# Column means of w1 from one summed block: three adds on GpSimd, one product per quarter, and a later load of w2

## The chip, the cores and the metric

The kernel runs on one core of a Trainium2 chip. The metric is the device time in microseconds (us), median of several runs; less is better. A core has TensorE (matrix products), VectorE, ScalarE, GpSimd, and SyncE, whose queue issues the DMAs of this kernel. In the profile they are called PE, DVE, ACT, POOL and SP (SPq for the queue); PEld is the loading of TensorE's weights.

## The reference

The program is a layer with a long convolution (part A) followed by a two-layer perceptron (part B), over 2048 tokens of 512 columns, in bf16:

```python
def _A_ref(q, k, v, shift_k, ssm_k, ssm_D):
    # k_shift: causal 4-tap filter of k; kv = k_shift * v
    # y: causal convolution of kv with ssm_k, 2048 long, by FFT of length 4096
    y = y + kv * ssm_D[None, None, :]
    return q * y
def _B_ref(x, w1, w2):                       # w1: 512 x 1376, w2: 1376 x 512
    h = jnp.maximum(jnp.einsum("bsd,df->bsf", x, w1), 0)
    return jnp.einsum("bsf,fd->bsd", h, w2)
x = A_q
h = x + _A_ref(_layernorm(x, axis=-1), A_k, A_v, A_shift_k, A_ssm_k, A_ssm_D)
h2 = h + _B_ref(_layernorm(h, axis=-1), B_w1, B_w2)
```

The second layernorm is not applied to h by the kernel. Its subtraction of the mean is moved into the weights: from each column of `w1` the mean of that column over the 512 rows is taken off. Its division is applied at the end, per token. The column means of `w1` are what this change is about.

## The kernel before

The convolution is done with matrix products: a two-stage forward transform of the filter and of kv, a product in the transformed domain, and a two-stage inverse. The span falls into these stretches:

- 0 to 30 us: loading, tables of sines, taps of k, first stages of the transforms.
- 30 to 61 us: second stage for the filter, first stage for kv.
- 61 to 92 us: `product(kp)` for 16 values of kp, each with `finish` two steps behind. VectorE and GpSimd share the multiplications (L452), ScalarE copies, TensorE combines them in `psy` (L462). The result is `kf`.
- 92 to 110 us: inverse stage 1, `inv1(b)` for b = 0 to 15. Each b is 16 small products (L609) into `psi`, which one engine then copies to `ax` (L259 on ScalarE, L261 on VectorE; VectorE has b = 5 and 10 and half of the last). `psi` has three places in PSUM, used in a ring, so block b can begin when the copy of block b-3 is done.
- From 110 us: inverse stage 2 (`inv2_first`, `inv2`, result `pz`), `gate` (times the normed x, plus x, L660 and L662), and the perceptron, `mlp1(sc)` (L716) and `mlp2(sc)` (L746) for four groups sc of 512 tokens. The products of `inv2` for the next groups are slipped in between those of `mlp1` and `mlp2`.

Each engine takes its instructions strictly in the order of the program, since the schedule is written by hand. The order of the calls in the text is thus the order of the queues. What stands around the change:

- `load_x(q)` brings the tokens of group q into `xh[q]`; `lift(q)` transposes them to `xT[q]` by DMA. `ln1_stats(q)` computes mean and variance of each token on VectorE (`st` L547, `mv` L551) and from it `rstd` in two steps on GpSimd (L553, L554). `ln1_norm(q)` applies both on VectorE in four instructions (`qln`, L571) and sends the result through a transposing DMA to `qT[q]`.
- `ec_turns(q)` computes angles on GpSimd (one iota, L526, and two multiplications, L529); `ec_wrap(q)` reduces them on VectorE (L533); sines of them on ScalarE give `ecore0` (for group 0) and `bd` (L537, for the others), both operands of inverse stage 2.
- `column_means(n)` for n = 0 to 3 multiplies a 128x128 block of 1/512 in bf16, `ones`, with a quarter of the columns of `w1` (344 of 1376). `w1` lies as four row blocks of 128 rows, so a quarter takes four products that add up in PSUM in `cen[n]` (tile `pm`, L497). n = 0 and 1 stand in front of inverse stage 1, n = 2 after b = 9, n = 3 after b = 15.
- `center` subtracts the means from `w1` (L578): quarters 0 and 1 on VectorE after b = 5, quarters 2 and 3 on GpSimd, which gets the means by way of `wm`.
- `load_w2` brings `w2` by two DMAs (L590, L592), after `lift(0)` and before inverse stage 1. `w2` takes the place of the table `c2n1`, which the last `product` reads last.

Of the kernel before, what the change touches and what calls it, by code (L numbers as in the profile page):

```python
# [9 lines left out]
ALU = mybir.AluOpType  # L10
BF16 = mybir.dt.bfloat16
F32 = mybir.dt.float32
F32R = mybir.dt.float32r
I32 = mybir.dt.int32
PSUM = bass.MemoryType.PSUM
P = 128
# [40 lines left out]
def kernel(  # L57
# [13 lines left out]
    nc = tc.nc  # L71
    _, S, D = A_q.shape
    DFF = B_w1.shape[1]
# [3 lines left out]
    DC = D // P  # L77
    NFC = (DFF + P - 1) // P
# [10 lines left out]
    wp = pl.push("wp", side="right")  # L89
# [49 lines left out]
    def _sin(out, turns, M, neg=False):  # L139

        nc.scalar.activation(out=out, in_=turns, func=ACT.Sin, scale=(-TURN if neg else TURN) / M,
                             bias=(pbias if neg else nbias)[:])
# [94 lines left out]
    for rg in range(DC):  # L237
        nc.gpsimd.tensor_tensor(out=wdiag[:, rg, :, :], in0=ident[:].unsqueeze(1).to_broadcast([P, KS, P]),
                                in1=wsh[:, rg, :].unsqueeze(2).to_broadcast([P, KS, P]), op=ALU.mult)
# [152 lines left out]
    ones = consts.tile([P, P], BF16, name="ones")  # L392
# [64 lines left out]
    def finish(at):  # L457
        kp, (tr, ti) = pending.pop(0)
        for s, (a, b, m) in enumerate(((tr[:, 0], ti[:, 1], ineg), (tr[:, 1], ti[:, 0], ipos))):
            psy = psy_.tile([P, 512], F32, tag=f"psy{s}", name=f"psy{s}")  # L460
            for m_, t_, first in ((ipos, a, True), (m, b, False)):
                nc.tensor.matmul(out=psy[:], lhsT=m_[:], rhs=t_.rearrange("p j k -> p (j k)"),  # L462
                                 start=first, stop=not first)
            copy("D" if at == 16 and s == 1 else "A", kf[:, s, :, 2 * kp:2 * kp + 2],
                 psy[:].rearrange("p (j k) -> p j k", k=2))
# [9 lines left out]
    for kp in range(16):  # L475
# [6 lines left out]
        if kp == 10:  # L482
            w1 = wp.tile([P, DC, DFF], BF16, tag="c2s0", name="w1")
# [5 lines left out]
    psum1 = pl.push("psC", space=PSUM)  # L489
    psum_a = pl.push("psIa", space=PSUM)  # L490
    FS = 344
    cen = {}

    def column_means(n):
        cen[n] = psum1.tile([P, 512], F32, tag=f"pm{n % 2}", name="pm")
        for c in range(DC):
            nc.tensor.matmul(out=cen[n][:, 0:FS], lhsT=ones[:], rhs=w1[:, c, n * FS:(n + 1) * FS],  # L497
                             start=(c == 0), stop=(c == DC - 1))

    while pending:  # L500
        finish(16)
    column_means(0)
    column_means(1)
    pl.pop("psY")
    places[:] = [psum_a] + [pl.push("psIb", side="right", space=PSUM)] * 2
    ring[:] = [0, 1, 2]
# [10 lines left out]
    rstd2 = late.tile([P, NT, 1], F32, name="rstd2")  # L517
    ecw = [late.tile([P, 2, 512], I32, name="ecw0"), wp.tile([P, 2, 512], I32, tag="c2s1", name="ecw1")]
    ecore0 = wp.tile([P, 2, 16, 32], F32R, tag="c2n0", name="ecore0")
    w2 = wp.tile([P, NFC, D], BF16, tag="c2n1", name="w2")  # L520
    bd = [late.tile([P, 2, 8, DC, 32], F32R, name="bd0")]
    act_pool = {0: late}

    def ec_turns(q):
        t = ecw[q % 2]
        nc.gpsimd.iota(t[:, 1, :].rearrange("p (i a n) -> p i a n", i=4, a=4), pattern=[[1, 4], [16, 4], [64, 32]],  # L526
                       base=4 * q, channel_multiplier=0)
        for rho, o in enumerate((2048 + 4096, 8192)):
            nc.gpsimd.tensor_scalar(out=t[:, rho, :], in0=t[:, 1, :], scalar1=k1o[:], scalar2=float(o),  # L529
                                    op0=ALU.mult, op1=ALU.add)  # L530

    def ec_wrap(q):
        nc.vector.tensor_single_scalar(out=ecw[q % 2][:], in_=ecw[q % 2][:], scalar=8191, op=ALU.bitwise_and)  # L533
# [22 lines left out]
    def rows_T(dst, src):  # L556
        nc.sync.dma_start_transpose(out=dst[:].rearrange("p i r t -> p (i r) t"),
                                    in_=src.rearrange("p i d -> p (i d)"))

    def lift(q):  # L560
        xT[q] = act_pool[q].tile([P, 4, DC, P], BF16, name=f"xT{q}")
        rows_T(xT[q], xh[q])

    def ln1_stats(q, part=slice(0, 4)):
        stats(xh[q], mv1, rstd1, q, part)

    def ln1_norm(q):
        qln = late.tile([P, 4, D], BF16, tag="qln", name="qln", bufs=1)
        for i in range(4):
            t = 4 * q + i  # L570
            nc.vector.tensor_scalar(out=qln[:, i, :], in0=xh[q][:, i, :], scalar1=mv1[:, t, 0:1],  # L571
                                    scalar2=rstd1[:, t, :], op0=ALU.subtract, op1=ALU.mult)
        qT[q] = act_pool[q].tile([P, 4, DC, P], BF16, name=f"qT{q}")
        rows_T(qT[q], qln[:])

    def center(eng, n, mean):
        fs = slice(n * FS, (n + 1) * FS)
        eng.tensor_tensor(out=w1[:, :, fs], in0=w1[:, :, fs], in1=mean.unsqueeze(1).to_broadcast([P, DC, FS]),  # L578
                          op=ALU.subtract)
# [4 lines left out]
    def off_center(n):  # L584
        nc.vector.tensor_copy(out=wm[:, n - 2, :], in_=cen[n][:, 0:FS])
        center(nc.gpsimd, n, wm[:, n - 2, :])

    def load_w2():
        nfull = DFF // P
        nc.sync.dma_start(out=w2[:, 0:nfull, :], in_=B_w2[0:nfull * P, :].rearrange("(c p) d -> p c d", p=P))  # L590
        if DFF % P:
            nc.sync.dma_start(out=w2[0:DFF % P, nfull, :], in_=B_w2[nfull * P:DFF, :])  # L592

    ec_turns(0)
    ln1_stats(0)
    ec_turns(1)
# [2 lines left out]
    def inv1(b):  # L599
        if b < 15:  # L600
            ps = bank2("psi1")
            banks = (ps[:, 0], ps[:, 1])
        else:
            banks = (psum1.tile([P, 512], F32, tag="pm0", name="psi1a")[:], bank2("psi1b")[:, 0, :])
        for i in range(4):
            m = 4 * b + i
            for c, tab in ((0, dre), (1, dim)):
                for dp in range(2):
                    nc.tensor.matmul(out=banks[dp][:, 128 * i:128 * i + 128],  # L609
                                     lhsT=kf[halves[dp], c, 4 * m:4 * m + 4, :].rearrange("p r k -> p (r k)"),  # L610
                                     rhs=tab[halves[dp], dp].rearrange("p a b -> p (a b)"), start=(c == 0), stop=(c == 1),
                                     tile_position=(64 * dp, 0), skip_group_check=True)
        if b < 15:
            copy("D" if b in (5, 10) else "A", ax[:, :, :, 4 * b:4 * b + 4],
                 ps[:].rearrange("p d (i x) -> p x d i", i=4))
        else:
            for dp, eng in enumerate("AD"):
                copy(eng, ax[:, :, dp, 60:64], banks[dp].rearrange("p (i x) -> p x i", i=4))

    lift(0)  # L620
    load_w2()
    ec_wrap(0)
    ln1_stats(1, slice(0, 2))
    for b in range(16):
        inv1(b)
        if b == 4:
            ln1_norm(0)
            _sin(ecore0[:].rearrange("p b j n -> p b (j n)"), ecw[0][:], 8192)
        if b == 5:
            center(nc.vector, 0, cen[0][:, 0:FS])  # L630
            ln1_stats(1, slice(2, 4))
            center(nc.vector, 1, cen[1][:, 0:FS])
        if b == 7:
            ec_turns(2)
        if b == 9:
            column_means(2)
        if b == 10:
            off_center(2)
            ec_wrap(1)
    column_means(3)  # L640
    nc.vector.tensor_copy(out=wm[:, 1, 1:FS], in_=cen[3][:, 1:FS])
    nc.vector.tensor_copy(out=wm0[:], in_=cen[3][:, 0:1])
    bd_sins(1, 0)
# [200 lines left out]
```

## Time and profile before

| what | value |
|---|---|
| median of 3 runs | 204.63 us (204.31 to 205.11) |
| profiled execution: its own time | 203.83 us |
| profiled execution: span from first to last instruction | 201.7 us |
| granted TensorE clock, mean | 0.995 |
| PE busy | 192.0 us, 95% of the span |
| DVE busy | 145.3 us, 72% |
| ACT busy | 128.5 us, 64% |
| POOL busy | 86.5 us, 43% |
| column means on PE, L497 | 16 products of 128x344, 91.8 to 109.3 us |
| centring on POOL, L578 | 2 of 128x1376, mean 2844 ns |
| centring on DVE, L578 | 2 of 128x1376, mean 1559 ns |
| rstd on POOL, L554 | 8, mean 1036 ns |
| w2's DMAs | issued at 95.7 and 96.5 us, 1280 and 96 KB |

The busy figures are averages over stretches with different limits. A busy time of PE includes products that are pipelined, so it does not say that PE works at its peak. What a change in one stretch is worth is read from the chain of work that ended last, in that stretch: it follows back, from the last instruction, what released each step.

### The profile page before, as it was taken

Reading aid. Unit: us, or ns where it says so; the run is one execution under the profiler, and the core shown is the slowest. Engines: PE = TensorE matmul, PEld = TensorE weight load, DVE = VectorE, ACT = ScalarE, POOL = GpSimd, SP = SyncE. Lnnn points to the kernel's source line nnn. Section 1 sums busy time; section 2 is a strip of 40 time slices with the busy share of each in tenths; the row PEclk is TensorE's granted clock in tenths of the full one; section 3 lists DMA queues with packets and bytes.
Section 4 is the critical chain, followed back from the end, with each engine's and each line's share of the span. In section 5 each row is a group of like instructions: output and inputs, shape, how many; then the busy total and the mean of one; then the engine's idle time right before and its main releaser. Section 6 shows DMA issues by size and latency. Waiting matters only on the chain.

```text
span 201.7 us, 5574 instructions
## 1 busy us (share of the span) xinstructions
PE 192.0 (95%) x2337; PEld 135.5 (67%) x2337; DVE 145.3 (72%) x238; ACT 128.5 (64%) x199; POOL 86.5 (43%) x121
## 2 busy tenths in 40 slices
PE   7799999999988999999999999999999999999991
PEld 2465555999977998987988877545664556544451
DVE  7998777887887998898994798968477127661131
ACT  2668899678785888885979865925570683036300
POOL 7599994000016999994959293301120002002000
PEclk9999999999999999999999999999999999999998
DMA  6999991000000007719981989744381702140011
GB/s 164 349 221 181 165 180 27 3 5 3 6 3 2 0 23 196 272 28 209 275 190 28 113 77 199 141 99 106 82 156 57 104 0 52 35 96 28 0 52 52
DMA packets 48492, 20.06 MB, mean 99 GB/s; under 512 B 43380, under 2 KB 46932, under 8 KB 48468
## 3 DMA queue, kind: packets, MB, share of 16 engines
q1 hardware_dynamic: 47940, 19.71, 48.1%
q8 instruction: 18, 0.29, 0.6%
q10 hardware_dynamic: 528, 0.00, 0.1%
q14 instruction: 6, 0.05, 0.1%
HBM read 7.08 MB, written 2.10 MB: 46 GB/s over the span
## 4 chain that ended last, share of the span: by engine, by line
PE 69%; SPq 10%; DVE 8%; DMA 5%; ACT 3%; issue 1%; POOL 1%; ACTq 0%
PE ps1m L716 19%; PE ps2m L746 19%; PE psy L462 6%; PE ps2k L328 4%; DMA kT<-in_A_k_dram 4%; SPq L115 4%; PE ps2k L330 4%; PE u L328 4%; PE u L330 3%; SPq L118 3%; SPq L117 3%; PE pz L689 3%; PE ps L310 2%; PE pst L281 2%; PE pkv L369 2%; DVE st L547 2%
## 5 line engine op out<-in xcount | busy, mean ns | idle before, releaser
L731 ACT ACTIVATE h1T<-ps1m 128x512 bf16<-128x512 f32 (+1 forms) x44 | 25.7, 597 | 35.8 <-PE ps1m L716 35.7
L716 PE MATMUL ps1m<-xT,w 128*128 128x512 bf16 (+2 forms) x192 | 43.7, 365 | 0.4 <-DVE xT L662 0.4
L746 PE MATMUL ps2m<-w,h1T 128*128 128x512 bf16 (+3 forms) x187 | 40.8, 368 | 0.0
L689 PE MATMUL pz<-bd,ax 128*128 128x128 f32 x96 | 35.7, 410 | 0.0
L452 POOL TENSOR_TENSOR t<-usb,kf 128x320 fp32r<-128x320 f32 x32 | 28.2, 930 | 2.2 <-ACT usb L448 1.7
L452 DVE TENSOR_TENSOR t<-u,kf 128x704 fp32r<-128x704 f32 x32 | 26.7, 884 | 3.3 <-ACT usb L448 3.2
L750 DVE SCALAR_TENSOR_TENSOR o<-ps2m,rstd,xh 128x512 bf16<-128x512 f32 (+1 forms) x17 | 12.1, 717 | 22.4 <-PE ps2m L746 11.5
L553 POOL TENSOR_SCALAR rstd<-mv 128x4 f32<-128x4 f32 x8 | 2.5, 317 | 57.1 <-DVE mv L551 57.1
L746 PEld LDWEIGHTS <-h1T 128*128 128x128 bf16 (+1 forms) x187 | 16.2, 98 | 16.0
L259 ACT CAST a<-ps 128x1024 fp32r<-128x1024 f32 (+1 forms) x22 | 22.4, 1053 | 2.8 <-PE ps L310 2.8
L716 PEld LDWEIGHTS <-w 128*128 128x128 bf16 (+1 forms) x192 | 15.9, 100 | 12.1 <-DVE xT L662 0.5
L689 PEld LDWEIGHTS pz<-bd,ax 128*128 128x128 f32 x96 | 18.6, 193 | 7.6
L547 DVE BATCH_NORM_STATS2 st<-xh 128x6 f32<-128x512 bf16 x32 | 19.9, 677 | 0.4 <-DMA xh<-xT 0.4
L660 DVE TENSOR_TENSOR qT<-pz,qT 128x1024 bf16<-128x1024 f32 x8 | 9.8, 1220 | 13.6 <-PE pz L689 10.8
L259 ACT CAST kf<-psy 128x512 fp32r<-128x512 f32 x30 | 17.5, 642 | 1.9 <-PE psy L462 0.2
L537 ACT ACTIVATE bd<-ecw,nbias 32x512 fp32r<-32x512 int32 x24 | 17.3, 719 | 0.6
L462 PE MATMUL psy<-t,ipos 128*128 128x512 f32 x48 | 16.0, 393 | 0.0
L369 PE MATMUL pkv<-kT,wdiag 128*128 128x512 bf16 x64 | 15.2, 380 | 0.6 <-POOL f_lo L247 0.4
L261 DVE CAST a<-ps 128x1024 fp32r<-128x1024 f32 (+1 forms) x12 | 13.6, 1136 | 2.7 <-PE ps L310 2.5
L259 ACT CAST ax<-psi 128x1024 fp32r<-128x1024 f32 x13 | 12.3, 1038 | 3.7 <-PE psi L609 3.5
L372 DVE TENSOR_TENSOR sk<-pkv,vT 128x512 bf16<-128x512 f32 x16 | 10.7, 689 | 4.5 <-PE pkv L369 4.1
L609 PE MATMUL psi<-dre,kf 64*128 64x128 f32 x120 | 13.8, 274 | 0.1
(132 smaller groups left out, 401.6 us busy)
## 6 DMA issues: line engine op xcount, KB each, us to landing
sk<-in_A_ssm_k_dram SPq DMA_DIRECT2D x1, 2048.0 KB
xh<-in_A_q_dram SPq DMA_DIRECT2D x16, 128.0 KB
out_dram<-o SPq DMA_DIRECT2D x15, 128.0 KB
w<-in_B_w_dram SPq DMA_DIRECT2D x1, 1376.0 KB
w<-in_B_w_dram SPq DMA_DIRECT2D x1, 1280.0 KB
xh<-xT SPq DMA_TRANSPOSE x8
out_dram<-o SPq DMA_DIRECT2D x2, 64.0 KB
w<-in_B_w_dram SPq DMA_DIRECT2D x1, 96.0 KB
```

The costliest lines, as they stand in the source:

```text
L259: nc.scalar.copy(out=o, in_=i)
L328: nc.tensor.matmul(out=ps[:, kk, :], lhsT=at_k1(w_re, k1), rhs=a_in(2 * k1), start=True, stop=False, skip_group_check=True)
L330: nc.tensor.matmul(out=ps[:, kk, :], lhsT=at_k1(w_im, k1), rhs=a_in(2 * k1 + 1), start=False, stop=True, skip_group_check=True)
L369: nc.tensor.matmul(out=pss[i][:], lhsT=wdiag[:, 2 * h + i, j, :], rhs=kT[c][:, 2 * h + i, 16 - j:CH + 16 - j], start=(j == 0), stop=(j == ...
L452: eng.tensor_tensor(out=t[:, :, j, :], in0=in0.unsqueeze(1).to_broadcast([P, 2, n, 2]), in1=kfr[:, :, j, ks], op=ALU.mult)
L462: nc.tensor.matmul(out=psy[:], lhsT=m_[:], rhs=t_.rearrange("p j k -> p (j k)"), start=first, stop=not first)
L537: nc.scalar.activation(out=bd[h][rows, :, :, rg, :], in_=ecw[q % 2][rows, :, 256 * h:256 * h + 256].rearrange("p b (j n) -> p b j n", n=32 ...
L547: nc.vector.bn_stats(out=st[:, i, :], in_=src[:, i, :])
L689: nc.tensor.matmul(out=pz[:, il, :, a, :], lhsT=ax[:, 64 * rho + n2, :, :].rearrange("p d g -> p (d g)"), rhs=bd[h][:, rho, 4 * il + a, :, ...
L716: nc.tensor.matmul(out=ps1[fc][:fsz, 128 * ii.start:128 * ii.stop].rearrange("p (i t) -> p i t", t=P), lhsT=w1[:, c, fc * P:fc * P + fsz], ...
L731: nc.scalar.activation(out=h1T[:fsz, fc, :], in_=ps1[fc][:fsz, :], func=ACT.Relu)
L746: nc.tensor.matmul(out=ps2[:, 0:w], lhsT=h1T[:ksz, fc, i * P:(i + 1) * P], rhs=w2[:ksz, fc, ds], start=(fc == 0), stop=(fc == NFC - 1))
```

## The change

The four row blocks of `w1` are added up on GpSimd into `wsum`, in fp32 (read by TensorE in its fp32r format), beside a copy `ones32` of `ones` in that format. Both lie in one tile in the place of `c2n1`. `column_means(n)` is then one product per quarter instead of four. The cast and the three adds stand on GpSimd in front of `ec_turns(0)`. `column_means(0)` and `(1)` move from in front of inverse stage 1 to after b = 5. The sine for `ecore0` moves behind b = 5, and `ec_wrap(0)` from in front of the stage to after `ln1_norm(0)` at b = 4. Since `w2` needs the place of `wsum`, its tile and `load_w2` move behind `column_means(3)`, at the end of the stage; on the queue of SP, its two DMAs go from behind `lift(0)` to between the transpose of `qT[0]` and `lift(1)`.

```diff
-    def column_means(n):
-        cen[n] = psum1.tile([P, 512], F32, tag=f"pm{n % 2}", name="pm")
-        for c in range(DC):
-            nc.tensor.matmul(out=cen[n][:, 0:FS], lhsT=ones[:], rhs=w1[:, c, n * FS:(n + 1) * FS],
-                             start=(c == 0), stop=(c == DC - 1))
     while pending:
         finish(16)
-    column_means(0)
-    column_means(1)
...
-    w2 = wp.tile([P, NFC, D], BF16, tag="c2n1", name="w2")
+    wsum1 = wp.tile([P, DFF + P], F32R, tag="c2n1", name="wsum")
+    wsum, ones32 = wsum1[:, 0:DFF], wsum1[:, DFF:DFF + P]
...
+    def column_means(n):
+        cen[n] = psum1.tile([P, 512], F32, tag=f"pm{n % 2}", name="pm")
+        nc.tensor.matmul(out=cen[n][:, 0:FS], lhsT=ones32, rhs=wsum[:, n * FS:(n + 1) * FS], start=True, stop=True)
...
+    nc.gpsimd.tensor_copy(out=ones32, in_=ones[:])
+    for c in range(1, DC):
+        nc.gpsimd.tensor_tensor(out=wsum, in0=w1[:, 0, :] if c == 1 else wsum.bitcast(F32), in1=w1[:, c, :], op=ALU.add)
     ec_turns(0)
     ln1_stats(0)
     ec_turns(1)
...
     lift(0)
-    load_w2()
-    ec_wrap(0)
     ln1_stats(1, slice(0, 2))
     for b in range(16):
         inv1(b)
         if b == 4:
             ln1_norm(0)
+            ec_wrap(0)
+        if b == 5:
+            column_means(0)
+            column_means(1)
             _sin(ecore0[:].rearrange("p b j n -> p b (j n)"), ecw[0][:], 8192)
-        if b == 5:
             center(nc.vector, 0, cen[0][:, 0:FS])
             ln1_stats(1, slice(2, 4))
             center(nc.vector, 1, cen[1][:, 0:FS])
...
     column_means(3)
+    w2 = wp.tile([P, NFC, D], BF16, tag="c2n1", name="w2")
+    load_w2()
```

## The prediction

> **What bounds the kernel now.** I read the page's busy table first, then the chain of waits in order of time, then the timelines of VectorE and GpSimd around the edit (90 to 116 us), because the edit lies in one short stage, inverse stage 1, and a whole-span average says little there. TensorE is busy 95% of the span and carries 69% of the chain, so fewer products look like a gain. The chain in order of time says that in this stage they are not:
>
> ```profile
> 95.15 0.29 DVE mv L551 x4
> 95.51 0.59 POOL rstd L553
> 96.17 1.06 POOL rstd L554
> 97.26 1.48 DVE qln L571 x3
> 98.82 0.39 DVE qln L571
> 99.22 1.13 DVE ax L261
> 100.35 1.49 DVE w L578
> ...
> 103.32 1.47 DVE w L578
> 104.79 1.15 DVE ax L261
> 105.98 1.13 PE psi L609 x16
> ```
>
> Columns: start, duration, engine, result, line. From 95 to 106 us the chain is on VectorE and GpSimd. GpSimd's `rstd` (ending at 97.22) releases `ln1_norm(0)` (four `qln`); behind it on VectorE's queue stands the copy `ax` of block b=5, which frees the PSUM place that block 8 needs (three places in a ring); then two centrings, and `ax` of b=10, which frees the place for block 13 (105.98). TensorE meets this chain with almost no slack: block 8 would follow block 7 at 100.18+0.11 and starts at 100.41. So every us by which `rstd` gets later is a us on the end. How GpSimd reaches `rstd`:
>
> ```profile
> 79.77 11.20 POOL L452 TENSOR_TENSOR t<-usb,kf 128x320 fp32r<-128x320 f32 x12
> 92.11 0.62 POOL L526 IOTA ecw<- 128x512 int32 x1 [1.14 <-PE psy L462]
> 92.83 1.49 POOL L529 TENSOR_SCALAR ecw<-ecw,k1o 128x512 int32<-128x512 int32 x2
> 95.51 0.58 POOL L553 TENSOR_SCALAR rstd<-mv 128x4 f32<-128x4 f32 x1 [1.19 <-DVE mv L551]
> 96.17 1.05 POOL L554 TENSOR_TENSOR rstd<-rstd,mhalf 128x4 f32<-128x4 f32 x1
> ```
>
> In brackets: the idle time before, and who ended it. The engine has two holes here, 1.14 and 1.19 us: 2.33 us of new work is all that it can take in front of `rstd`.
>
> **What the Trainium skill says.** "GPSIMD Engine Reference", section 3.1 "Elementwise — side-by-side cycle accounting": a two-input `tensor_tensor` is held by one shared read port, and 2048 fp32 columns took 4497 ns. Scaled to 1376 columns this is an estimate of 3.02 us. The trace agrees: GpSimd's centring, two inputs and 1376 columns, takes 2.84 us. "SBUF — State Buffer", section "SBUF: two separate sides": a GpSimd operation and a VectorE operation in a 2-port mode exclude each other for a whole instruction. The trace agrees: the first `qln` of `ln1_norm(1)`, usually 0.40 us, took 2.91 beside that centring at 116.06. "TensorE: Matmul & The Clock Gate", part 1: after an idle window of about 3.4 us the clock falls to half. No window of before shows TensorE idle for so long; its clock is 1.00 throughout this stage.
>
> **The change, part by part.**
>
> *Removed: 12 of 16 mean products.* Four take 0.76 us with the last one's drain, so about 0.15 us each; 12 are 1.8 us. The eight ahead of inverse stage 1 held it from 91.83 to 93.09, but block 0 also needs the last `kf` copy on VectorE, which ends at 92.77. It then begins at about 92.85: 0.24 us earlier, and this vanishes at block 8, which waits for VectorE. The three saved at b=9 are before block 13, which waits for VectorE too. The last three are beside the closing copy of b=15 (to 109.64), which `pz` waits for. Gain on the path: none. The four fp32r products left cost as much as bf16 ones: the identity products at L462 stream 512 fp32 columns every 0.23 us, so 344 take 0.16.
>
> *Added on GpSimd, ahead of `ec_turns(0)` and so of `rstd`:* one 128x128 cast and three adds over 1376 columns. The cast: 0.30 us, from the same shape at L432. An add: mixed bf16 and fp32 input with fp32 output is not in the trace. Nearest rows: the centring (2.84), and L452 at 0.912 us for 320 columns, which per column gives 3.92 as an upper end since its fixed part is scaled too. Lower end 2.7, if the narrower first operand helps. I take 2.95, between 2.84 and the page's 3.02. `w1` was asked for at 79.32 and the queues are empty from 86 to 88, so the adds need not wait for it; the cast's place (`c2n1`) was last read by the products at 89.1.
>
> Start at 90.97 (end of L452) + 0.05; cast to 91.3; 3 x 2.95 + 3 x 0.07 between dependent instructions: 100.35. Then `ec_turns(0)`, 2.21 us (92.11 to 94.32): 102.6. Then `rstd`, 1.36 us where nothing was waited for (103.41 to 104.77): 103.95, against 97.22. **The wait at `qln` grows by 6.7 us.** Statistics of x(0) and half of x(1) are done by then; nothing else on VectorE can pass.
>
> *Moved on VectorE:* `ec_wrap(0)`, in the shadow of `rstd` before, now stands between `qln` and `ax` of b=5. It costs 0.66 us undisturbed and 1.10 where it met L529 at 119.96; GpSimd is again at L529 and a memset then. I take 0.9. **Block 8 starts 7.6 us later**, at about 108.0. Ends for this sum: 6.5 (a=2.7, 0.66) to 11.0 (a=3.92, 1.10).
>
> *The new wait on TensorE:* the products 0 and 1 stand after b=5 (done at 98.3) and wait for the sum at 100.4. Blocks 6 and 7 are queued behind them, done at 102.5; then TensorE idles until 108.0. The 2 us are inside the larger wait, so they cost nothing.
>
> *ScalarE:* the sine of `ecore0` moves only relative to the wrap: it waits until about 107.6 for `ec_wrap(0)`, with the copies of b=6 to 9 behind it, one each 0.95 us. That puts b=9's copy at 112.5, before the 113.6 at which `ax` of b=10 ends (5.6 us after that of b=5, as before). It hides by about a us.
>
> *w2.* Its two DMAs leave SP's queue ahead of `qT` and go behind the last mean product, at about 109+7.6. `qT`(0) gets a free queue; it was not late. Behind the load now stand `lift(1)` and the transposes of the gates. Issuing costs SP 0.72+1.17 us, and 1.38 MB at the 349 GB/s seen from 100 to 102 us costs 4 us of queue. Counted in before's times (shift taken off): w2 done at 113.5, `xT`(1) at 118 instead of 114, the first `xh` at 122, `qT`(1) at about 125.5 instead of 124.6. `gate(1,0)` so starts some 1 us late; `gate(1,1)` ended at 131.7 and TensorE asks for it at 135.7. w2 itself is wanted at 127.3. Cost 0, with 4 us of cover.
>
> *Sum:* 203.83 (profiled execution: a span of 201.7 and 2.1 around it) + 7.6 = 211.4. The profiled execution was 0.80 below the median shown (204.63), so against the median: **212.2 us**.
>
> **The rivals.**
>
> *Later costs on top (B).* TensorE idle for 5.5 us may drop to half clock. Blocks 8 to 11 would then take 1.8 us instead of 0.9; VectorE's 4.4 us between the two `ax` copies hide two of the extra 0.9s, so 0.5 to 2 us remain. Or the transposes behind w2 use up more than the 4 us. For it: the idle stretch is long. Against: VectorE paces this stage. 213.8 to 216.5.
>
> *Cheaper adds (C).* If GpSimd adds contiguous columns at about the rate of its memset (2048 columns in 1.81 us, so 1.2 us for 1376) up to 2.3 us, the shift is 7.6 - 3 x (2.95 - a), that is 2.3 to 5.7: 207 to 210.3. Against: every two-input row.
>
> *Faster (D).* The sum falls into GpSimd's idle 2.33 us and TensorE sheds its 1.8 us: 202.8. This asks for (2.33 - 0.3 - 0.2)/3 = 0.6 us per add at the most, a fifth of the nearest row, and for a stage paced by TensorE. Even then `ec_wrap` would take 0.7 back. The page's 95% for TensorE speaks for it, the chain against it.
>
> That the change doesn't do what it says I give nothing: the order of instructions on each engine has the adds in front of `ec_turns(0)`, and four products for sixteen.
>
> **How the numbers follow.** Forecast (A) 0.68; B 0.20; C 0.09; D 0.03. A's own range is 211 to 214. With the whole stretch of B and the upper part of C, 209.0 to 216.5 leaves out under 2 in 10. About 0.5% (1 us) is what a measurement of this kernel can tell from no change: slower by more holds for A, B and C, 0.96; the rest I halve, 0.02 within 0.5% and 0.02 faster.
>
> **What would show it.** Right: three adds of 2.8 to 3.1 us on GpSimd ending near 100.4; `rstd` idle-free and ending near 104; the chain through them; VectorE idle some 7 us before `qln`; TensorE idle some 5.5 us before block 8; everything from `pz` on shifted by 7 to 8 us with the same gaps. Wrong: adds under 2 us; `ax` of b=5 not following `qln`; a TensorE clock under 0.9 in the slice after the gap (B); a wait of `mlp1(1)` for `xT` or of `mlp2(0)` for `w2` (B, through the queue).

## The result, and the profile after

The changed kernel takes 219.38 us (median of 6 runs, 219.04 to 220.42) against 204.70 before: a ratio of 1.073, 95% interval 1.0701 to 1.076. That is 14.7 us slower, where 7.6 was forecast and 216.5 was the upper end of the range. The profiled execution took 219.31 us, with a span of 217.5.

The direction was right, and the mechanism in the first half too. The chain of work that ended last, in order of time (start, duration, engine, result, line; L546 and L547 are `rstd`, L564 `qln`, L526 `ec_wrap`, L680 `pz`):

```profile
91.61 2.77 POOL wsum L593
...
94.45 2.82 POOL wsum L593
...
97.34 2.80 POOL wsum L593
100.15 0.58 POOL ecw L519
...
102.72 1.06 POOL rstd L547
...
104.43 1.34 DVE qln L564 x3
105.76 1.02 DVE ecw L526
106.78 1.14 DVE ax L261
...
107.97 3.67 PE psi L609 x24
...
112.22 8.72 PE psi L609 x41
...
123.56 6.08 PE pz L680 x111
```

The adds, the angles, `rstd`, `qln`, the wrap and the copy of b=5 follow each other without a hole, and block 8 starts at 107.97; 108.0 was forecast. Of these 7.6 us, 0.4 lie before the edit in this execution (the table below). VectorE's timeline shows the new wait, and the wrap behind it (in brackets: idle time before, and who ended it):

```profile
103.81 1.96 DVE L564 TENSOR_SCALAR qln<-xh,mv,rstd 128x512 bf16<-128x512 bf16 x4 [6.72 <-POOL rstd L547]
105.69 1.10 DVE L526 TENSOR_SCALAR ecw<-ecw 128x1024 int32<-128x1024 int32 x1
```

TensorE has two idle stretches, one ahead of the first mean product and one ahead of block 8:

```profile
100.20 0.59 PE L583 MATMUL pm<-wsum 128*128 128x344 f32 x2 [1.50 <-POOL wsum L593]
...
107.97 0.47 PE L609 MATMUL psi<-dre,kf 64*128 64x128 f32 x2 [3.91 <-DVE ax L261]
```

The second was forecast at 5.5 us. It is shorter because blocks 6 and 7 in front of it were already slow, and this is what the forecast left out: the clock. The clock lines of the pages (40 slices, 5.0 us each before and 5.4 after, in tenths of full speed; 9 is 90% or more) show it, before and after:

```profile
PEclk9999999999999999999999999999999999999998
```

```profile
PEclk9999999999999999997555569999999999999999
```

TensorE runs at half clock through the rest of inverse stage 1 and most of the first `pz`. Three rows of the table of stretches show when (the stretch and its length, the busy time of PE, PEld, DVE, ACT and POOL with the number of instructions, then the granted clock, the DMA share and GB/s):

```profile
100.00:102.00 2.00, 1.80 (x18) 1.58 (x18) 0.00 (x0) 0.00 (x0) 1.80 (x4) 0.78 0.00 0
...
112.00:114.00 2.00, 2.00 (x19) 1.85 (x18) 0.35 (x1) 0.70 (x1) 1.81 (x4) 0.50 0.00 0
...
128.00:130.00 2.00, 1.75 (x54) 1.67 (x51) 1.97 (x3) 1.08 (x2) 0.00 (x0) 0.89 1.80 301
```

If the clock falls once in a stretch, a mean of 0.78 over 2 us means 0.88 us at half clock, so it fell at about 101.1; by the same working it was back at 128.4. From 112 to 122 TensorE is busy without a pause and the clock stays at 0.50.

Cutting both profiles at the same events gives the account of the 15.8 us of span (us; "fill" is experiment e7 below):

| stretch | before | after | difference | fill |
|---|---|---|---|---|
| start to end of the products on GpSimd (L452) | 90.97 | 91.37 | +0.4 | 92.37 |
| to block 8 | 9.44 | 16.60 | +7.2 | 17.33 |
| block 8 to `pz` | 9.37 | 15.59 | +6.2 | 8.77 |
| `pz` to the first product of `mlp1` | 4.27 | 6.31 | +2.0 | 4.69 |
| to the end | 87.65 | 87.63 | 0.0 | 87.54 |

The first row lies before the edit; the end of these products ranges from 90.8 to 93.0 us over the twelve profiles. The second row is the forecast, 7.2 us against 7.6. Rows three and four, 8.3 us together, are the part that was missed.

### The profile page after: what moved, and what is told of

Same layout as the page of the kernel before. It is cut to its first block, busy times and chain, and to the rows that moved or that the text cites. A ratio compares the mean times of both kernels' runs of the same rounds, so it can differ in the third digit from the quotient of the medians.

```text
span 217.5 us, 5542 instructions
## 1 busy us (share of the span) xinstructions
PE 201.1 (92%) x2312; PEld 145.2 (67%) x2325; DVE 145.3 (67%) x238; ACT 129.0 (59%) x199; POOL 94.3 (43%) x125
## 4 chain that ended last, share of the span: by engine, by line
PE 74%; POOL 10%; DMA 7%; DVE 4%; ACT 2%; issue 1%; DVEq 0%; POOLq 0%; ACTq 0%
PE ps1m L719 18%; PE ps2m L749 17%; PE psi L609 6%; PE psy L462 5%; PE ps2k L328 4%; DMA wsh<-in_A_shift_k_dram 4%; POOL wsum L593 4%; PE pkv L369 4%; PE ps2k L330 3%; PE ps L310 3%; PE pz L692 3%; PE u L328 3%; PE pz L680 3%; DMA vT<-in_A_v_dram 3%; PE u L330 3%; POOL wdiag L238 2%
## 5 line engine op out<-in xcount | busy, mean ns | idle before, releaser
L749 PE MATMUL ps2m<-w,h1T 128*128 128x512 bf16 (+3 forms) x181 | 40.2, 368 | 0.2
L452 POOL TENSOR_TENSOR t<-usb,kf 128x320 fp32r<-128x320 f32 x32 | 28.2, 937 | 2.2 <-ACT usb L448 1.7
L452 DVE TENSOR_TENSOR t<-u,kf 128x704 fp32r<-128x704 f32 x32 | 26.7, 890 | 3.2 <-ACT usb L448 3.2
L546 POOL TENSOR_SCALAR rstd<-mv 128x4 f32<-128x4 f32 x8 | 2.2, 275 | 55.9 <-DVE mv L544 55.8
L609 PE MATMUL psi<-dre,kf 64*128 64x128 f32 x120 | 20.3, 355 | 4.2 <-DVE ax L261 3.9
L609 PE MATMUL psi<-dim,kf 64*128 64x128 f32 x120 | 20.1, 354 | 0.3 <-DVE kf L261 0.3
L663 DVE TENSOR_TENSOR qT<-pz,qT 128x1024 bf16<-128x1024 f32 x8 | 9.8, 1221 | 15.6 <-PE pz L692 10.8
L609 PEld LDWEIGHTS psi<-dre,kf 64*128 64x128 f32 x120 | 16.2, 267 | 5.3 <-DVE ax L261 4.1
L609 PEld LDWEIGHTS psi<-dim,kf 64*128 64x128 f32 x120 | 16.3, 270 | 0.4 <-DVE kf L261 0.4
```

The costliest lines, as they stand in the source:

```text
L452: eng.tensor_tensor(out=t[:, :, j, :], in0=in0.unsqueeze(1).to_broadcast([P, 2, n, 2]), in1=kfr[:, :, j, ks], op=ALU.mult)
L609: nc.tensor.matmul(out=banks[dp][:, 128 * i:128 * i + 128], lhsT=kf[halves[dp], c, 4 * m:4 * m + 4, :].rearrange("p r k -> p (r k)"), rhs= ...
L749: nc.tensor.matmul(out=ps2[:, 0:w], lhsT=h1T[:ksz, fc, i * P:(i + 1) * P], rhs=w2[:ksz, fc, ds], start=(fc == 0), stop=(fc == NFC - 1))
```

## The experiments

All kernels were timed against the kernel before on the same chip.

**e4_adds: the adds alone.** The kernel before, with its sixteen mean products where they were, and only the GpSimd work added; the load of `w2` has to make room.

```diff
+    nc.gpsimd.tensor_copy(out=ones32, in_=ones[:])
+    for c in range(1, DC):
+        nc.gpsimd.tensor_tensor(out=wsum, in0=w1[:, 0, :] if c == 1 else wsum.bitcast(F32), in1=w1[:, c, :], op=ALU.add)
     ec_turns(0)
...
     column_means(3)
+    w2 = wp.tile([P, NFC, D], BF16, tag="c2n1", name="w2")
+    load_w2()
```

> The kernel before with the cast and the three adds on GpSimd in front of the angles of group 0, and the later load of w2 that the place of the sum asks for; sixteen mean products where they were, the sum is read by nobody. Theory 1 (the adds in front of rstd make the whole loss): qln starts at about 104, block 8 at about 107.3 (no wrap in the way), one idle stretch of TensorE of about 7 us, clock at half after it, time 217.5 to 219.5. Rival (the mean products' place after b=5 and their wait for the sum matter): clock stays up, time 211 to 212.5.

Measured: 219.42 us, ratio 1.0728 (1.0694 to 1.0761), the same as the whole change. `qln` started at 104.86 and block 8 at 108.00, some 0.8 us later than expected (L452 ended at 91.91, 0.9 us later than before), one idle stretch of 6.6 us before it, and the clock fell at about 103.6. So the adds in front of `rstd` are enough for a loss of this size. The rest of the change, that is the twelve products saved, their wait for the sum and the later wrap, adds nothing to the total that can be measured. By stretches it does show: e4, with its wrap in front of `qln`, needs 0.5 us less from the end of L452 to block 8 (16.1 against 16.6), and 1.0 us more from there to `pz` (16.6 against 15.6). At half clock its four products for a mean take 1.33 us on TensorE, where the one product of the changed kernel takes 0.65.

**e1_both and e3_second: fillers that came too late.** Products whose results nobody reads, meant for the idle stretches of TensorE; `FS:512` are the unused columns of a bank that holds means.

```diff
+            filler = psum1.tile([P, 512], F32, tag="pm0", name="filler")
+            for _ in range(8):            # e1 only, ahead of column_means(0)
+                nc.tensor.matmul(out=filler[:], lhsT=xh[0][:, 0, 0:P], rhs=xh[0][:, 1, :], start=True, stop=True)
...
         if b == 7:
+            for _ in range(52):           # 40 in e3
+                nc.tensor.matmul(out=cen[0][:, FS:512], lhsT=xh[0][:, 0, 0:P], rhs=xh[0][:, 1, 0:512 - FS],
+                                 start=True, stop=True, skip_group_check=True)
```

> The changed kernel, with filler products whose results nobody reads in TensorE's two idle stretches: 8 of 128x512 bf16 ahead of the first mean product, 52 of 128x168 bf16 between blocks 7 and 8. Theory 1 (the idle stretches drop TensorE's clock to half and that costs the second half of the loss): clock 1.00 throughout, block 8 at about 108 as in the changed kernel, inverse stage 1 done near 116.5 instead of 122.7, time 211.5 to 213. Rival (what comes after block 8 is lost to waits: ring places, the sine on ScalarE, w2's queue; the clock is only a symptom): 218.5 to 220.

> The changed kernel with fillers in the second idle stretch only (40 products of 128x168 bf16 between blocks 7 and 8). Theory 1: the clock falls at about 101 as in the changed kernel, the fillers bring it back by 106, time 211.5 to 214.5. If dense bf16 products don't bring it back: 218 to 221. Rival (waits): 218.5 to 220 whatever the clock.

Measured: 218.08 us, ratio 1.0659 (1.0641 to 1.0677) for e1; 217.78, ratio 1.0649 (1.0626 to 1.0673) for e3. TensorE's timeline of e1:

```profile
99.05 1.67 PE L630 MATMUL filler<-xh 128*128 128x512 bf16 x7 [0.16 <-issue]
100.88 0.56 PE L583 MATMUL pm<-wsum 128*128 128x344 f32 x2
...
109.67 5.79 PE L639 MATMUL pm<-xh 128*128 128x168 bf16 x52 [6.30 <-DVE w L571]
```

The second set waited for VectorE's centring (L571), which reads the same tile, and ran after the idle stretch instead of in it. The runs still tell something: the clock was back at about 113.6 in both, some 4 us after the dense bf16 products began, and from block 8 (115.38 in e1) to `pz` (124.15) it took 8.8 us instead of 15.6. The kernel e1 does 5.7 us of useless work on the path, and is still 1.3 us faster than the changed kernel. Neither theory's range was met (e1 lies below that of the waits, e3 below that of a clock that stays down). The result speaks for the clock as the cause of the second half, but the kernels were not the ones meant.

**e2_first: only the short idle stretch filled.** The first `+` lines of e1 alone.

> The changed kernel with fillers in the first idle stretch only (8 products of 128x512 ahead of the first mean product). Theory 1a (the long stretch of 5.5 us before block 8 is enough to drop the clock): the clock falls inside it, after 103, and stays at half to about 128; time 217.5 to 219.5. Theory 1b (the short stretch of 1.8 us is what drops it, since in the changed kernel it fell at about 101, before the long one): clock stays at 1.00, time 211.5 to 213.5. Rival (waits): 218.5 to 220, with the same clock as in the changed kernel.

Measured: 219.08 us, ratio 1.0722 (1.0697 to 1.0748). With the first stretch filled the clock held until about 106.2, inside the long one (102.6 to 107.4), and came back at about 126.6. This is theory 1a. The short stretch (98.7 to 100.2 in the changed kernel) went ahead of the fall there, but the long one is enough for it; filling the short one alone buys nothing.

**e7_fill: both stretches filled in time.** The fillers of the long stretch go into the bank of the second mean, ahead of that product, so that nobody reads it yet.

```diff
+    def fill(tag, n):
+        t = psum1.tile([P, 512], F32, tag=f"pm{tag}", name="filler")
+        for _ in range(n):
+            nc.tensor.matmul(out=t[:], lhsT=xh[0][:, 0, 0:P], rhs=xh[0][:, 1, :], start=True, stop=True)
         if b == 5:
+            fill(0, 8)
             column_means(0)
+            _sin(ecore0[:].rearrange("p b j n -> p b (j n)"), ecw[0][:], 8192)
+        if b == 7:
+            fill(1, 24)
             column_means(1)
-            _sin(ecore0[:].rearrange("p b j n -> p b (j n)"), ecw[0][:], 8192)
             center(nc.vector, 0, cen[0][:, 0:FS])
...
-        if b == 7:
             ec_turns(2)
```

> The changed kernel with filler products nobody reads in both idle stretches, now into a bank that nothing else reads yet, so that they wait for nothing: 8 of 128x512 bf16 ahead of the first mean product, 24 between blocks 7 and 8; the second mean product moves behind them. Theory 1 (idle TensorE drops the clock, half clock in inverse stage 1 and the products after it costs the 7 us that the delay of block 8 leaves unexplained): clock 1.00 throughout, block 8 at 107.5 to 108.5, pz 9 us after it, time 211.5 to 213. Rival (waits after block 8: sine, ring places, w2's queue): pz 13 us or more after block 8 at any clock, time over 217.

Measured: 212.32 us, ratio 1.0356 (1.0331 to 1.0381). TensorE's timeline (the profile has 23 of the 24 products) and the clock line of its page:

```profile
103.93 5.35 PE L588 MATMUL filler<-xh 128*128 128x512 bf16 x23
109.35 0.42 PE L583 MATMUL pm<-wsum 128*128 128x344 f32 x1
```

```profile
PEclk9999999999999999999999999999999999999999
```

This is the experiment that decides. TensorE does more work than in the changed kernel, VectorE still waits 6.73 us for `rstd`, and the time falls by 7.1 us (by the ratios, 7.7). In the table above the stretches after block 8 are back at the lengths of before (8.77 and 4.69 us). So the rival, waits behind block 8, falls. What is left, 7.5 us, is the forecast's own sum of 7.6.

Block 8 itself came at 109.70 and not by 108.5 as expected: 1.0 us of that lies before the edit (92.37 against 91.37), and the fillers end about 0.7 us after VectorE's copy (108.9). The stretch after it is 0.6 us shorter than before, so this hardly reaches the end.

**e6_half: half the adds.** The adds run over the first 688 columns; the means of quarters 0 and 1 stand in for those of 2 and 3.

```diff
-        nc.gpsimd.tensor_tensor(out=wsum, in0=w1[:, 0, :] if c == 1 else wsum.bitcast(F32), in1=w1[:, c, :], op=ALU.add)
+        nc.gpsimd.tensor_tensor(out=wsum[:, 0:2 * FS], in0=w1[:, 0, 0:2 * FS] if c == 1 else wsum[:, 0:2 * FS].bitcast(F32),
+                                in1=w1[:, c, 0:2 * FS], op=ALU.add)
```

> The changed kernel with the adds over the first 688 columns only; the means of quarters 0 and 1 stand in for those of 2 and 3. Adds of 1.4 to 1.5 us each, so rstd ends near 99.7 and block 8 starts 3.2 to 3.5 us later than before, after one idle stretch of about 3.3 us. Theory 1 with a stretch that is too short to drop the clock: 207.5 to 208.5. Theory 1 with a clock that falls: 213 to 216. Rival (each us on rstd costs two, by waits): 211 to 212.

Measured: 215.59 us, ratio 1.052 (1.0492 to 1.0549). The adds took 1.50 to 1.54 us, `qln` started at 99.86, block 8 at 104.02. TensorE was idle for 2.9 us before it, from 101.13, and the clock fell at about 104.4:

```profile
104.00:106.00 2.00, 1.98 (x22) 1.98 (x24) 2.00 (x3) 2.00 (x4) 0.58 (x1) 0.60 0.89 164
```

Block 8 is 3.6 us later than before, 0.4 of it from before the edit, as expected. From there to `mlp1` it takes 21.6 us against 13.6 before, so another 8.0 us follow at half clock. The delay is about in proportion to the adds (3.2 and 7.2 us), and the loss by the clock is not (8.0 and 8.3 us): once the clock has fallen, most of the stage runs at half of it in both kernels.

**e5_w2: w2 moved alone.**

```diff
-    load_w2()
...
     column_means(3)
+    w2 = wp.tile([P, NFC, D], BF16, tag="c2n1", name="w2")
+    load_w2()
```

> The kernel before with the load of w2 moved behind the last mean product and nothing else. Prediction's step (4 us of cover for what queues behind it): 204 to 205. Rival (the queue costs something): 205.5 or more, with a wait of mlp1(1) for xT or of mlp2(0) for w2.

Measured: 204.95 us, ratio 1.0004 (0.9988 to 1.0021). It tests only half of the move: `w2` now stands behind `qT` on SP's queue, but with no sum in its place it is issued at 102.5. That its being issued at the end of the stage costs nothing either is seen in e7 and in the changed kernel (issued at 123.3 there), where the stretch from `mlp1` to the end has the length of before (87.54 and 87.63 against 87.65 us).

**e8_late: the adds behind rstd.** e4 with its four GpSimd instructions after the zeroing of `bd[0]`.

> The kernel before with the same cast and adds on GpSimd (sum read by nobody) and the same later load of w2, but behind rstd of x(0), the angles of group 1 and the zeroing of bd, instead of in front of it. Theory 1 (a us of GpSimd costs only where VectorE waits for rstd): block 8 where it was, clock 1.00, and only the later GpSimd work is pushed back by 9 us (rstd of x(1), centring of quarters 2 and 3): 204.5 to 207, with a wait of mlp1(0) for the centred quarter 2 if it is more than 205. Rival (the adds cost by contention with VectorE or by GpSimd's time as such): 210 or more.

Measured: 220.67 us, ratio 1.0793 (1.0762 to 1.0824), so the expectation failed. VectorE's timeline:

```profile
100.08 1.21 DVE L261 CAST ax<-psi 128x1024 fp32r<-128x1024 f32 x1
111.14 1.59 DVE L579 TENSOR_TENSOR w<-w,pm 128x1376 bf16<-128x1376 bf16 x1 [9.85 <-POOL wsum L601]
```

The copy of b=5 is on time now, but the centring behind it writes `w1`, which the adds still read. It waits 9.85 us with the copy of b=10 behind it, TensorE idles for 9.4 us, and the clock falls. The rival is not shown by this: it is the same loss by another wait. The sum thus has to be read out of `w1` before the first centring, and `rstd` has to be early too.

**r1_order and r2_order: other orders for the same work.** In r1 the copy of b=5 goes ahead of `qln`, that of b=10 to ScalarE, the first means after b=8. In r2 further steps move, to remove the waits that r1 still had.

```python
        inv1(b)                                   # r2, its order
        if b == 8:
            column_means(0)
            column_means(1)
            center(nc.vector, 0, cen[0][:, 0:FS])
            ln1_norm(0)
            ec_wrap(0)
            center(nc.vector, 1, cen[1][:, 0:FS])
        if b == 12:
            column_means(2)
            nc.vector.tensor_copy(out=wm[:, 0, :], in_=cen[2][:, 0:FS])
...
```

> The changed kernel with its adds where they are and the queues reordered so that TensorE waits for nothing behind rstd: the copy of b=5 goes ahead of qln on VectorE, the copy of b=10 goes to ScalarE, the first two mean products follow b=8, the sine of ecore0 goes to the end of the stage, the second half of the statistics of x(1) behind it. If the loss is the place of rstd in VectorE's queue and not the adds' own 9 us: block 8 at 100 to 101, clock 1.00, time 203.5 to 206. If the adds cost by themselves (shared memory ports, angles and zeroing that come later on GpSimd): 207 or more.

> The changed kernel reordered once more: copy of b=5 ahead of qln and copy of b=10 on ScalarE as in r1, first mean products after b=8, but qln and the wrap between the two centrings, the sine ahead of b=14's copy, block 15 in a place of the ring instead of the bank of the means, bd's second zeroing and the centring of quarter 2 ahead of the angles of group 2, and the second half of the statistics of x(1) after the first gate. Theory 1: no idle stretch of TensorE over 0.7 us in inverse stage 1, clock 1.00, pz within 0.7 us of the kernel before: 203.5 to 205.5, so at best even with before. Rival (1.8 us of products saved would show once nothing waits): under 203.5. If a new wait appears as in r1: 206 to 209.

Measured: 210.10 us, ratio 1.0249 (1.0226 to 1.0273) for r1; 208.48, ratio 1.019 (1.0165 to 1.0215) for r2. Both miss the time that was hoped for (203.5 to 206, 203.5 to 205.5). In both, block 8 no longer waits for `rstd`. In r1 TensorE waits 0.74 us ahead of block 15, 0.62 ahead of `pz` and 1.76 in `mlp1`, and the clock is down from about 111.2 to 118.0. In r2 TensorE goes through inverse stage 1 without a stop, and then waits 2.1 us ahead of `pz` (109.40 to 111.54). The wait moved to the end of the stage: `qln` and the wrap come at 104 to 107, the sine of `ecore0` only at 108.2, and the last copies on ScalarE behind it. The clock fell again (at about 111.1) and was back by 114.6. Compared with the kernel before, r2 needs 1.1 us more from the end of L452 to `pz`, 1.3 more from there to `mlp1`, and 1.3 more from `mlp1` to the end, where a new wait of 1.35 us stands in `mlp1`. Several things move at once in these two, but they fit the first cause from the other side: with the adds in place and `rstd` off the path to block 8, 4.0 of the 14.7 us are left. No order that was tried beats the kernel before.

## Why the prediction was wrong in its size

- **Bound by `rstd` and not by products: right.** e4 has all sixteen products and the same time as the changed kernel. It holds at full clock; at half clock TensorE sets the pace.
- **The cost of the adds: right.** 2.82 to 2.85 us on GpSimd's timeline (2.95 taken), `ec_turns(0)` 2.21 us, cast 0.31. `qln` started at 103.81, 6.6 us later than before (6.7 forecast). VectorE's idle time of 6.72 us is not quite the same thing: it also holds the 0.66 us that the wrap took there before. The wrap took 1.10 us, its upper bound (0.9 taken).
- **Block 8, and the time without the rest: right.** 107.97 us against 108.0; e7, which keeps only this part, takes 212.32 us against 212.2. That the first agrees to 0.03 us is luck: counted from the end of L452 the delay is 7.2 us and not 7.6, since the adds were somewhat cheaper, and the 0.4 from before the edit make up for it.
- **The products saved, the wait for the sum, the sine, w2: right at 0 while the clock is full** (e4, e5, e7, and the last row of the table). At half clock the products saved do count, by up to 1 us (e4).
- **The clock: seen, and mis-sized.** This is the step that failed. The forecast itself puts the clock at nothing, and rival B has "Blocks 8 to 11 would then take 1.8 us instead of 0.9; VectorE's 4.4 us between the two `ax` copies hide two of the extra 0.9s, so 0.5 to 2 us remain." It put the chance at 0.20 and its end at 216.5. The block time was about right: copies of `ax` follow each other every 1.71 us. The duration was not. The working counts four blocks at half clock and gives no reason for the clock to be back after them; it stayed at half through all blocks that were left, and through most of `pz`, from 101.1 to 128.4. Blocks 8 to 15 and `pz` cost 8.3 us more by the profile; the fillers of e7 bring back 7.1 us by the medians. B's range of 213.8 to 216.5 is also more than 0.5 to 2 us on top of 212.2; the rest would have to come from the transposes behind w2, which cost nothing.
- **The argument against B was wrong as well.** "VectorE paces this stage" holds at full clock. At half clock TensorE takes 1.71 us for a block, VectorE and ScalarE wait for it (VectorE 6.31 us ahead of its last copy), and the bound has changed sides.
- The short wait for the sum was called free, since it lies inside a larger wait. In time it was; but in the changed kernel the clock fell 2.4 us after it began, and with it filled (e2) not before 106.2. e2 also shows that this made no difference to the end.
- Slips on which nothing rests: by its own terms the ends of the sum for block 8 are 6.6 and 10.7 us, not 6.5 and 11.0; and the `qln` of 2.91 us beside the centring is the second of `ln1_norm(1)`, from 116.16, not the first.

The Trainium skill, "TensorE: Matmul & The Clock Gate", part 1, gives an idle window of about 3.4 us for the fall and a busy one of the same length for the return. Here 1.5 us of idle time were followed by the fall, and 14.6 us of products without a pause did not bring the return, while the bf16 fillers of e1 and e3 brought it in about 4 us. The measurement decides.

## What to carry to other kernels

Before work is put on an engine that is "43% busy", ask what stands behind it in its queue and who waits for that: here 9 us on GpSimd became 7.5 us on TensorE, through one small `rstd`, while the 1.8 us saved on TensorE were not on the path. Then ask where TensorE will stand still, since the stall can have a second price that depends on what runs next: here that work did not raise the clock by itself, and the price lasted as long as the work did. A cheap test for it is filler products in the idle stretch, into a bank that nobody reads; look in the timeline that they ran there.

## What the runs showed of the hardware

- **A short stall can be followed by a fall of the clock, and its length alone does not tell.** Working from tables of stretches as above, the clock fell 2.4 us after the start of a stall of 1.5 us (changed kernel), 1.7 us after the start of one of 0.74 us (r1) and of one of 2.1 us (r2), 3.3 us after the start of one of 2.9 us (e6), and 2.2 us after the start of one of 6.6 us (e4). All these stand in inverse stage 1 or at its end. In all twelve kernels TensorE also waits 1.47 to 1.48 us ahead of the products of 128x256 at L328, a wait that ends between 60.9 and 63.0 us, and there the clock stays at 1.00. The same holds for the stalls of 1.76 us (r1) and 1.35 us (r2) in `mlp1`. What decides was not tried. The kernel before has no stall over 0.41 us between 90 and 120 us and no fall there.
- **Not every dense stream brings it back.** Inverse stage 1 (64-row fp32r products of 128 columns) held full clock while it was warm, and at half clock did not recover in 14.6 us. The bf16 fillers brought it back in about 4 us (e1, e3). In the kernels with one product per mean it was back 3.0 us (r2) to 5.6 us (e6) after `pz` began, whose fp32r products lie in four groups of 32 rows; in the changed kernel after 4.9 us. At half clock the weight loads of inverse stage 1 take 330 ns instead of 188 and its products 412 instead of 272. Why this stage keeps the clock but cannot raise it was not tried.
